# First batch of a packed attention and expert layer: the copy of T ahead of the gates' steps, row logits and guess one item back each

## The chip, the cores and the metric

One core of a Trainium2 chip runs the kernel. The metric is the device time of one execution in microseconds (us), lower is better. The engines are TensorE (PE, matmuls; PEld is its weight load), VectorE (DVE), ScalarE (ACT), GpSimd (POOL) and SyncE (SP, which issues most transfers). Each runs its instructions in the order in which the program gives them, and waits where an operand is not ready.

## The reference

Two attentions in a row, then a layer of experts. 32 packing queries `p` of each head attend to keys and values and give 32 packed rows; the queries `q` attend to these rows. The result (8 batches of 576 tokens, 512 wide) goes through a router that picks one of eight experts per token.

```python
p_packed = sm_attn(p, k, v)
out = sm_attn(q, p_packed, p_packed)
...
xn = x / (np.linalg.norm(x, axis=-1, keepdims=True) + 1e-06)
logits = xn @ en.T / tau
expert_idx = np.argmax(logits, axis=1)
gate_w = probs[np.arange(N), expert_idx]
h = np.maximum(x[mask] @ w1[e], 0.0)
out[mask] = gate_w[mask, None] * (h @ w2[e])
```

## The kernel before

The kernel works batch by batch (b = 0 to 7, 576 tokens each). For each batch it guesses one expert for all tokens, from the logits of the packed rows; it counts afterwards how many tokens chose another, and a loop at the end, which the drawn inputs do not enter, would handle those.

Attention of a batch: key scores, exponential, turning of the probabilities (`p1_turn`), packed rows (`pack_values`, L381), then two masked forms of these rows on DVE (`pair_rows`, `quad_rows`, L393). The pairs are turned on PE (`pair_turn`, L410) and **DVE copies them to T** (L474, in `att1`). T feeds three things on PE: the **row logits** (`row_logits`, L424), whose result DVE copies to m1 (L434), the **guess** (`guess`, L507: m1 with 1/tau), whose argmax DVE finds (L511 to L516) and which lets POOL issue the loads of the expert's weights (L730, L738), and the query scores (`query_scores`, L251). `att2` is the softmax on them: transposes (L547), largest (L552), shift (L558), exponential on ACT (L561), sum (L567), norm (L573), turning (L582), high and low half (L588 on ACT, L592 on DVE). After it DVE turns the next batch's keys (`keys`, L276 to L293). `route` (L644 on PE, L653 on DVE, L660 on ACT) gives the token's logits and the square of its norm, in five tiles that share two PSUM buffers `pt`; `counts` (L686, L691) counts the experts chosen.

`gates` turns a batch's norms and logits into a gate per token. It is a generator: four groups of three small DVE steps (the reciprocal square root, L89 to L108, then two closing steps, L703 and L704, in the fourth), then L706, L707, the exponential on ACT (L711), L714, L715, L717, L719. The gates are needed by the stores (`store_main`, L1139 on ACT, then the transfers of L1145).

`ffn` is the expert: first product (L840), rows of the last 64 tokens (L868), third product (L884: for each of four blocks of 128 tokens, eight steps f of three matmuls 128x512), each step followed by a `yield`. In the first batch a table of strings, `PLAN`, says what is put between these steps: item n+1 is run after yield n. In an item, a letter runs one step of a generator: `a` one step of the attention of batch 1, `g` one step of the gates of batch 0 (the first one starts them), `r` one of its route (nothing once that is over), `w` the split of a piece of the second weights. Items 28 to 35, which the change rewrites, stand around the first six steps f of the third product's first block: item 29 is run after f = 0, item 30 after f = 1, and so on. With items 30 and 31 the second masked rows of batch 1 are turned, T is copied, row logits and guess run and the query scores begin.

Batches 1 to 7 do not use the table; there a rule of steps per yield sets the order.

Of the kernel before, what the change touches and what calls it, by code (L numbers as in the profile page):

```python
# [23 lines left out]
def kernel(  # L24
# [1109 lines left out]
    def store_main(b):  # L1134
# [32 lines left out]
    PLAN = (  # L1167
        "qssq", "sssssssssq", "ssqsssG", "ss", "", "ss", "sa", "asss", "a", "Gsq",
        "ss", "", "a", "aswGG", "aa", "as", "w", "aw", "ag", "qaawas",
        "awa", "g", "", "", "arwrw", "", "ara", "arraar", "ararrrgw", "",  # L1170
        "gaa", "agaaaag", "", "ragraaararga", "a", "gar", "gr", "", "rggr", "r",
        "ra", "", "r", "gag", "gaga", "gagrar", "grara", "ag", "a", "grrgrar",
        "rrraggg", "", "g", "rr", "ggaaagr", "ra", "aaga", "g", "r", "rg",
        "arr",
# [75 lines left out]
    with tc.If(n_rest > 0):  # L1250
        with tc.For_i(0, B, 1) as b:
            nb = nc.values_load(rest_i[0:1, ds(b, 1)], min_val=0, max_val=S)
            with tc.If(nb > 0):
# [44 lines left out]
                for c in range(NC5):  # L1298
                    for hf in range(2):
                        a = acc[hf][:, c] if c < 4 else acc[0][64 * hf : 64 * hf + 64, 4]  # L1300
# [38 lines left out]
```

## Time and profile before

| | |
|---|---|
| median of 3 runs | 451.07 us (450.13 to 451.11) |
| the profiled execution | 450.72 us, of it span 449.0 us |
| PE busy | 433.0 us, 96% of the span, 3762 instructions |
| DVE busy | 307.9 us, 69%, 1020 instructions |
| ACT busy | 203.6 us, 45%, 477 instructions |
| POOL busy | 144.8 us, 32%, 184 instructions |
| granted clock of TensorE | 0.999 of full speed (2.4 GHz) on the mean |

The profile is one execution, with a start and a duration for each instruction, and for idle time what ended it. Starts are in us from the span's start. A timeline merges instructions of one kind that follow each other, so a row "x27" is 27 instructions. Successive instructions of an engine overlap a little in these records where they do not depend on each other. PE's matmuls are pipelined and their ends are modelled; the start of the next one tells more than the end of the last.

### The profile page before, as it was taken

How to read it: one execution, taken by the hardware profiler on the slowest of the kernel's cores; microseconds unless marked ns; L12 is line 12 of the kernel's file. 1: busy time of each engine (PE TensorE's matmuls, PEld its weight loads, DVE VectorE, ACT ScalarE, POOL GpSimd, SP SyncE). 2: the span in 40 equal slices, each digit the busy share in tenths (PEclk: the TensorE clock that was granted, in tenths of full speed). 3: DMA queues.
4: the chain of work that ended last, by engine and by line, in shares of the span. 5: the costliest groups of instructions: out<-in, count | busy, mean ns of one | idle time of the engine just before them, and what ended most of it. 6: DMA issues, size and time to landing. Idle time of an engine off the chain costs nothing.

```text
span 449.0 us, 10448 instructions
## 1 busy us (share of the span) xinstructions
PE 433.0 (96%) x3762; PEld 340.6 (76%) x3763; DVE 307.9 (69%) x1020; ACT 203.6 (45%) x477; POOL 144.8 (32%) x184
## 2 busy tenths in 40 slices
PE   8789989999999999999999999999999999999994
PEld 6527768788687878878687887879788796879784
DVE  4568879669874799459894699658894598545500
ACT  2456723575137622475226642377234751456111
POOL 2546723143404432143503423044411525035000
PEclk9999999999999999999999999999999999999999
DMA  7999979866993479933995289944898305600011
GB/s 207 283 262 296 232 208 324 260 157 183 307 333 107 129 212 368 269 104 109 294 361 166 77 215 317 295 124 112 237 391 224 97 1 187 247 26 23 15 47 53
DMA packets 40843, 88.22 MB, mean 196 GB/s; under 512 B 10376, under 2 KB 19912, under 8 KB 40784
## 3 DMA queue, kind: packets, MB, share of 16 engines
q1 hardware_dynamic: 32496, 57.96, 45.4%
q0 software_dynamic: 8000, 29.43, 17.9%
q8 instruction: 32, 0.52, 0.5%
q14 instruction: 27, 0.22, 0.2%
q10 hardware_dynamic: 288, 0.08, 0.1%
HBM read 78.00 MB, written 9.44 MB: 195 GB/s over the span
## 4 chain that ended last, share of the span: by engine, by line
PE 84%; DMA 5%; ACT 3%; DVE 3%; issue 2%; SPq 1%; ACTq 0%
PE pf L884 40%; PE pf L840 19%; PE pf L868 7%; PE pt L644 7%; PE pt L251 4%; PE pt L773 3%; PE pt L381 3%; DMA nat<-in_q 2%; ACT p L346 2%; DMA nat<-in_v 2%; DMA w1t<-in_moe_w 1%; PE pt L361 1%; DVE mx L341 1%; ACT w2s L748 1%; SPq L730 1%
## 5 line engine op out<-in xcount | busy, mean ns | idle before, releaser
L884 PE MATMUL pf<-w2s,hT 128*128 128x512 f32 (+1 forms) x792 | 188.3, 390 | 0.0
L884 PEld LDWEIGHTS pf<-w2s,hT 128*128 128x128 f32 x792 | 142.5, 188 | 37.7 <-issue 6.7
L749 POOL TENSOR_TENSOR w2s<-w2r,w2s 128x512 fp32r<-128x512 f32 x64 | 82.6, 1292 | 188.4 <-ACT w2s L748 187.6
L840 PE MATMUL pf<-AT,G 128*128 128x288 f32 x720 | 103.4, 298 | 0.0
L840 PEld LDWEIGHTS pf<-AT,G 128*128 128x128 f32 x720 | 97.4, 188 | 4.5 <-issue 3.3
L844 ACT ACTIVATE hT<-pf 128x224 fp32r<-128x224 f32 (+1 forms) x128 | 47.6, 385 | 48.4 <-PE pf L840 47.9
L845 DVE SCALAR_TENSOR_TENSOR hT<-pf,hT 128x224 fp32r<-128x224 f32 (+1 forms) x128 | 52.0, 410 | 18.7 <-ACT hT L844 18.2
L660 ACT ACTIVATE at<-pt 128x512 f32<-128x512 f32 (+1 forms) x40 | 23.9, 597 | 42.9 <-DVE lg L653 42.6
L748 ACT CAST w2s<-w2r 128x512 fp32r<-128x512 f32 x64 | 39.6, 620 | 1.2 <-issue 1.2
L1139 ACT ACTIVATE o<-pf,gate 128x512 f32<-128x512 f32 (+1 forms) x41 | 26.0, 634 | 30.9 <-PE pf L884 18.6
L644 PEld LDWEIGHTS pt<-ppx,AT 128*128 128x128 f32 (+1 forms) x240 | 33.0, 177 | 4.4 <-DVE p1T L375 0.4
L644 PE MATMUL pt<-ppx,AT 128*128 128x264 f32 (+1 forms) x240 | 35.4, 286 | 0.0
L868 PE MATMUL pf<-w2r,h 128*64 128x256 f32 x256 | 33.9, 390 | 0.0
L653 DVE TENSOR_REDUCE lg<-pt 128x8 f32<-128x16 f32 (+1 forms) x40 | 6.8, 171 | 38.2 <-PE pt L644 38.2
L281 DVE STREAM_TRANSPOSE kt<-nat 128x512 f32<-128x512 f32 x28 | 30.9, 1104 | 0.1
L787 DVE TENSOR_TENSOR G<-pt,G 128x512 fp32r<-128x512 f32 x28 | 18.8, 689 | 14.2 <-ACT G L786 14.2
L266 POOL TENSOR_TENSOR ppx<-pp,ppx 128x256 fp32r<-128x256 f32 x16 | 11.7, 754 | 40.4 <-ACT ppx L265 40.4
L561 ACT ACTIVATE st<-st 128x576 f32<-128x576 f32 (+1 forms) x17 | 11.2, 657 | 29.0 <-DVE st L558 28.3
L868 PEld LDWEIGHTS pf<-w2r,h 128*64 128x64 f32 x256 | 15.8, 136 | 9.9 <-issue 4.3
L738 POOL DMA_DIRECT2D w2r<-in_moe_w x28 | 19.7, 711 | 0.0
L588 ACT CAST AT<-at 128x576 fp32r<-128x576 f32 x16 | 10.7, 673 | 19.6 <-DVE at L582 19.6
L786 ACT CAST G<-pt 128x512 fp32r<-128x512 f32 x28 | 15.8, 588 | 7.1 <-DVE G L787 4.8
(172 smaller groups left out, 479.6 us busy)
## 6 DMA issues: line engine op xcount, KB each, us to landing
nat<-in_k SPq DMA_DIRECT2D x112, 140.0 KB, 3.4
nat<-in_q SPq DMA_DIRECT2D x112, 140.0 KB, 3.8
w1t<-in_moe_w POOLq DMA_DIRECT2D x14, 1024.0 KB, 7.6
w2r<-in_moe_w POOLq DMA_DIRECT2D x28, 512.0 KB, 10.4
out<-o SPq DMA_DIRECT2D x27, 256.0 KB, 2.7
nat<-in_v SPq DMA_DIRECT2D x32, 160.0 KB, 4.1
nat<-in_v SPq DMA_DIRECT2D x32, 128.0 KB, 4.0
w1t<-in_moe_w SPq DMA_DIRECT2D x8, 256.0 KB, 4.6
```

What stands on the lines that cost most here:

```text
L281: nc.vector.transpose(kt[:, :512].rearrange("p (c i a) -> p c a i", a=4, i=32), t[:, :16].rearrange("p (c a) d -> p c a d", a=4),)
L644: nc.tensor.matmul(pt[:r, 512 * g : 512 * g + XW], AT[:, a, g, c * P : c * P + r], x.ppx[:, m, g], start=(i == 0), stop=(i == 2),)
L660: nc.scalar.activation(scr[:r, :, : HB * D], ptv[:r, :, 0 : HB * D], AF.Square, accum_out=ss[:r, c : c + 1])
L738: queue.dma_start(t, w2e[:, 2 * i : 2 * i + 2, :])
L748: nc.scalar.copy(t[:, 0], raw)
L749: nc.gpsimd.tensor_tensor(out=t[:, 1], in0=raw, in1=t[:, 0].bitcast(F32), op=ALU.subtract)
L840: nc.tensor.matmul(pf[:, :HS], w, r, start=(n == 0), stop=(n == len(ops) - 1))
L844: nc.scalar.activation(hT[:, 0, f, cs], pf[:, :n], AF.Relu)
L845: nc.vector.scalar_tensor_tensor(out=hT[:, 1, f, cs], in0=pf[:, :n], scalar=0.0, in1=hT[:, 0, f, cs].bitcast(F32), op0=ALU.max, op1=ALU.su ...
L868: nc.tensor.matmul(pf[64 * hf : 64 * hf + 64, :256], h4[:, f], x.w2r[f // 2][:, f % 2, hf * 256 : hf * 256 + 256], start=(f == 0), stop=(f ...
L884: nc.tensor.matmul(pf[:, :w], hT[:, a, f, c * P : (c + 1) * P], x.w2s[f][:, m, at : at + w], start=(f == 0 and i == 0), stop=(f == NF - 1 ...
L1139: nc.scalar.activation(o[:, :w], pf[:, :w], AF.Copy, scale=x.gate[:, c : c + 1])
```

## The change

Items 28 to 35 of `PLAN` are rewritten. The number of `a` and `g` steps in the table stays the same, and no instruction is added or removed. The gates' first step moves from item 28 to item 32, the second from 30 to 33. The `a` steps that copy T stay in item 30; row logits move from item 31 to 32, guess and query scores from 31 to 33, and the softmax steps follow in 33 to 35.

```diff
-        "awa", "g", "", "", "arwrw", "", "ara", "arraar", "ararrrgw", "",
-        "gaa", "agaaaag", "", "ragraaararga", "a", "gar", "gr", "", "rggr", "r",
+        "awa", "g", "", "", "arwrw", "", "ara", "arraar", "ararrrw", "",
+        "aa", "", "ag", "aaag", "agaaaaga", "gaaa", "gr", "", "rggr", "r",
```

On PE, between the turning of the pairs (L410) and the rest of the third product's first block (L884), the order differs as follows (- before, + changed); `pu` holds the row logits and the guess, `pt` the query scores:

```order
-L884 MATMUL pf<-w2s,hT 128x512 x3
-L424 MATMUL pu<-enT,T 64x8 x4
-L507 MATMUL pu<-m_1015,itau 1x8 x2
-L251 MATMUL pt<-kt,T 32x288 x16
-L884 MATMUL pf<-w2s,hT 128x512 x69
+L884 MATMUL pf<-w2s,hT 128x512 x6
+L424 MATMUL pu<-enT,T 64x8 x4
+L884 MATMUL pf<-w2s,hT 128x512 x3
+L507 MATMUL pu<-m_1008,itau 1x8 x2
+L251 MATMUL pt<-kt,T 32x288 x16
+L884 MATMUL pf<-w2s,hT 128x512 x63
```

Six matmuls of the third product instead of three stand ahead of the row logits, three more between these and the guess, and six fewer behind the query scores.

On DVE, at the same place, from the counts of the first batch on, before (`rq_i`, `rq_h`, `rq_t` and `gy` are the gates' steps, `m_1015` is m1):

```order
L691 TENSOR_REDUCE cnt<-pu 1x8
L89 TENSOR_SCALAR rq_i<-ss 128x5
L93 TENSOR_SCALAR rq_i<-rq_i 128x5
L98 TENSOR_SCALAR rq_h<-ss 128x5
L103 TENSOR_TENSOR rq_t<-rq_h,rq_i 128x5
L105 TENSOR_TENSOR rq_t<-rq_t,rq_i 128x5
L108 SCALAR_TENSOR_TENSOR gy<-rq_t,rq_i 128x5
L474 COPY T<-pu 128x256
L434 COPY m_1015<-pu 128x16
L103 TENSOR_TENSOR rq_t<-rq_h,gy 128x5
L105 TENSOR_TENSOR rq_t<-rq_t,gy 128x5
L108 SCALAR_TENSOR_TENSOR gy<-rq_t,gy 128x5
```

And in the changed kernel, from the same counts to the argmax:

```order
L691 TENSOR_REDUCE cnt<-pu 1x8
L474 COPY T<-pu 128x256
L434 COPY m_1008<-pu 128x16
L89 TENSOR_SCALAR rq_i<-ss 128x5
L93 TENSOR_SCALAR rq_i<-rq_i 128x5
L98 TENSOR_SCALAR rq_h<-ss 128x5
L511 MAX m_1024<-pu 1x8
L512 MAX_INDEX idx<-m_1024,pu 1x8
L514 CAST gi<-idx 1x1
L516 TENSOR_SCALAR sel<-ecol,gi 1x8
L103 TENSOR_TENSOR rq_t<-rq_h,rq_i 128x5
L105 TENSOR_TENSOR rq_t<-rq_t,rq_i 128x5
```

The copies of T and m1 now stand directly behind the counts, ahead of all of the gates' steps; one group of three of those goes behind the score transposes.

On DVE, at the end of the gates, in the softmax of batch 1, before (`s_1099` and `mx_1094` are sums and largest values of the softmax):

```order
L706 RECIPROCAL gy<-gy 128x5
L707 TENSOR_TENSOR lg<-lg,gy 128x40
L567 TENSOR_REDUCE s_1099<-st 128x18
L568 TENSOR_SCALAR s_1099<-s_1099 128x18
L569 RECIPROCAL s_1099<-s_1099 128x18
L558 TENSOR_TENSOR st<-st,mx_1094 128x576
L714 TENSOR_REDUCE gate<-lg 128x5
L715 TENSOR_SCALAR gate<-gate 128x5
L573 TENSOR_TENSOR st<-st,s_1099 128x576
L717 RECIPROCAL gate<-gate 128x5
L719 COPY gate<-gate 64x1
```

And in the changed kernel (`s_1102` and `mx_1095` are the same two):

```order
L567 TENSOR_REDUCE s_1102<-st 128x18
L568 TENSOR_SCALAR s_1102<-s_1102 128x18
L569 RECIPROCAL s_1102<-s_1102 128x18
L558 TENSOR_TENSOR st<-st,mx_1095 128x576
L573 TENSOR_TENSOR st<-st,s_1102 128x576
L706 RECIPROCAL gy<-gy 128x5
L707 TENSOR_TENSOR lg<-lg,gy 128x40
L714 TENSOR_REDUCE gate<-lg 128x5
L715 TENSOR_SCALAR gate<-gate 128x5
L717 RECIPROCAL gate<-gate 128x5
L719 COPY gate<-gate 64x1
```

The reduction L714, which waits for ACT's exponential of `lg`, follows L707 directly, where four softmax steps stood between them; on ACT that exponential (L711) moves behind the second one of the softmax (L561). From the turning of the first half (L582) on, the order on DVE is the same in both, the keys of batch 2 ahead of the route reductions (L653) included; on SP nothing moves.

## Rows read from the trace of the kernel before

**Rows 1.** The waits of PE over the whole span: who waited for what, us in total, times, longest.

```profile
PE pu L424 <- DVE T L474: 1.1, 1, 1.1
PE pu L507 <- DVE m L434: 0.3, 1, 0.3
```

**Rows 2.** The timeline of PE from 61.75 to 66 us: start, us, engine, line, operation, tiles, count, and in brackets the idle time before it and what ended it.

```profile
61.75 0.38 PE L410 MATMUL pu<-ident,pp 128*128 128x128 f32 x2
61.89 0.95 PE L884 MATMUL pf<-w2s,hT 128*128 128x512 f32 x3
63.94 0.41 PE L424 MATMUL pu<-enT,T 128*64 128x8 f32 x8 [1.10 <-DVE T L474]
64.62 0.24 PE L507 MATMUL pu<-m,itau 128*1 128x8 f32 x4 [0.28 <-DVE m L434]
```

**Rows 3.** The timeline of DVE from 61.4 to 74 us, with the same columns.

```profile
61.44 0.18 DVE L691 TENSOR_REDUCE cnt<-pu 1x8 f32<-1x40 f32 x1
61.54 0.15 DVE L89 TENSOR_SCALAR rq_i<-ss 128x5 int32<-128x5 int32 x1
61.73 0.74 DVE L93 TENSOR_SCALAR rq_i<-rq_i 128x5 int32<-128x5 int32 x1
...
62.58 0.58 DVE L103 TENSOR_TENSOR rq_t<-rq_h,rq_i 128x5 f32<-128x5 f32 x1
...
63.47 0.42 DVE L474 COPY T<-pu 128x256 f32<-128x256 f32 x1
64.39 0.17 DVE L434 COPY m<-pu 128x16 f32<-128x16 f32 x1 [0.51 <-PE pu L424]
...
66.19 0.84 DVE L547 STREAM_TRANSPOSE st<-pt 128x288 f32<-128x288 f32 x2
...
67.11 0.17 DVE L704 TENSOR_SCALAR gy<-gy 128x5 f32<-128x5 f32 x1
...
73.94 0.76 DVE L582 STREAM_TRANSPOSE at<-st 128x576 f32<-128x576 f32 x1
```

**Rows 4.** Two lines of the gates on DVE over the whole span, from the view of one source line: count, then shortest, median and longest duration in ns.

```profile
L93 DVE TENSOR_SCALAR rq_i<-rq_i x9: 99/172/745, 9.7 to 417.8; 128x5 int32<-128x5 int32 x8, 8x1 int32<-8x1 int32 x1
...
L103 DVE TENSOR_TENSOR rq_t<-rq_h,rq_i x8: 165/166/578, 62.6 to 418.0; 128x5 f32<-128x5 f32 x8
```

**Rows 5.** The timeline of POOL in the first batch's stretch, and its weight issues in the next batch (last row).

```profile
61.70 1.43 POOL L266 TENSOR_TENSOR ppx<-pp,ppx 128x256 fp32r<-128x256 f32 x2 [1.03 <-ACT ppx L265]
...
67.08 1.58 POOL L730 DMA_DIRECT2D w1t<-in_moe_w  x2 [1.96 <-DVE gy L703]
68.65 2.83 POOL L738 DMA_DIRECT2D w2r<-in_moe_w  x4
...
114.86 1.51 POOL L730 DMA_DIRECT2D w1t<-in_moe_w  x2 [2.20 <-DVE rq_t L105]
```

**Rows 6.** The timeline of DVE from 78 to 84 us: the low half of the second part of the softmax, and the first route reduction behind the keys.

```profile
78.67 0.76 DVE L592 TENSOR_TENSOR AT<-at,AT 128x576 fp32r<-128x576 f32 x1 [0.74 <-ACT AT L588]
...
83.01 0.17 DVE L653 TENSOR_REDUCE lg<-pt 128x8 f32<-128x16 f32 x1
```

**Rows 7.** The timeline of ACT: the gates' exponential, the first route tile's square with the reading of its sum, and the reading of the fourth one's.

```profile
70.70 0.24 ACT L711 ACTIVATE lg<-lg 128x40 f32<-128x40 f32 x1 [1.25 <-DVE lg L707]
...
83.77 0.19 ACT L660 ACTIVATION_READ_ACCUMULATOR at<-pt 128x1 f32 x1
...
87.36 0.19 ACT L660 ACTIVATION_READ_ACCUMULATOR at<-pt 128x1 f32 x1
```

**Rows 8.** The timeline of PE from 75.8 to 90 us: the third product's end, the route tiles (L644) and the first product's rows of the next batch (L773).

```profile
75.80 6.44 PE L884 MATMUL pf<-w2s,hT 128*128 128x512 f32 x27
82.08 1.63 PE L644 MATMUL pt<-ppx,AT 128*128 128x264 f32 x12
...
84.24 0.90 PE L644 MATMUL pt<-ppx,AT 128*128 128x264 f32 x6
...
87.61 1.95 PE L773 MATMUL pt<-w1t,T 64*32 64x512 f32 x32 [0.33 <-ACT at L660]
```

**Rows 9.** The timeline of DVE in the second batch, from 113 to 117 us: the guess's MAX, gate steps, and the gate reduction.

```profile
113.10 0.15 DVE L511 MAX8 m<-pu 1x8 f32<-1x8 f32 x1
...
113.87 0.15 DVE L103 TENSOR_TENSOR rq_t<-rq_h,gy 128x5 f32<-128x5 f32 x1
...
114.45 0.17 DVE L103 TENSOR_TENSOR rq_t<-rq_h,gy 128x5 f32<-128x5 f32 x1
...
114.85 0.17 DVE L108 SCALAR_TENSOR_TENSOR gy<-rq_t,gy 128x5 f32<-128x5 f32 x1
...
115.25 0.35 DVE L704 TENSOR_SCALAR gy<-gy 128x5 f32<-128x5 f32 x1
...
116.42 0.20 DVE L714 TENSOR_REDUCE gate<-lg 128x5 f32<-128x40 f32 x1 [0.36 <-ACT lg L711]
```

**Rows 10.** The waits of PE from 84 us to the end of the span, all that this view shows, in the form of rows 1.

```profile
PE pt L361 <- ACT p L346: 2.1, 6, 0.4
PE pt L773 <- ACT at L660: 0.3, 1, 0.3
```

**Rows 11.** The longest standstill of PE on a weight transfer, in the timeline, and the stretch of 26 to 28 us in the table of stretches (stretch, its length, then busy us and instructions of PE, PEld, DVE, ACT and POOL, granted clock, share of the transfer engines, GB/s).

```profile
28.27 1.05 PE L808 MATMUL pf<-w1t,tw 64*32 64x512 f32 x4 [1.29 <-DMA w1t<-in_moe_w]
...
26.00:28.00 2.00, 0.98 (x6) 0.07 (x4) 1.97 (x4) 1.61 (x4) 0.94 (x2) 1.00 1.00 340
```

## Prediction

> **What bounds the kernel now.** I read the waits of TensorE (PE) first, then the chain and timelines of the stretch that the change touches. PE is busy 96% of the span, so time comes out of its waits or nowhere. Two of these lie together in the first batch: 1.1 us in which the row logits wait for the copy of T, and 0.3 us in which the guess waits for the copy of m1 [rows 1]. The timeline shows the place: between the turning of the pairs and the query scores PE does three matmuls, then stands still [rows 2]. VectorE (DVE) was the late one: after the counts it ran six gate steps before the copy of T, which began at 63.47 [rows 3], although the turned pairs were there at 61.75 + 0.38 = 62.13 [rows 2]. Two of the six were slow, 0.74 and 0.58 us [rows 3], against medians of 0.17 over the run [rows 4]; GpSimd (POOL) was running its own split from 61.70 to 63.13 [rows 5].
>
> The second thing to see is twenty microseconds on. From the query scores DVE runs softmax, gates and the turning of the next batch's keys almost without a pause, and only then, at 83.01, the reduction of the first route tile [rows 6]. ScalarE (ACT) squares that tile up to 83.77 + 0.19 = 83.96 [rows 7], and the third route tile on PE, which takes over its buffer, starts at 84.24 [rows 8]. In the kernel before, PE comes there 0.28 us after the buffer is free. DVE is thus nearly the bound of this stretch, though PE looks full.
>
> **What PE gains.** No instruction is added or taken away; PE's row logits go behind two more steps of the third product, the guess behind one more. At the rate of 27 matmuls from 75.80 to 82.08 [rows 8], 0.233 us each, six take 1.40 us from 61.89: the row logits start at 63.29, after T is there (62.13 + 0.04 + 0.42 = 62.59). The handover of 0.04 is that from the row logits' end to the copy of m1, 64.35 to 64.39 [rows 2, 3]. Both waits of PE go: 1.10 + 0.28 = 1.38 us. PE therefore reaches the first route tiles at about 80.7 instead of 82.08.
>
> **What DVE pays.** The same instructions run, but with other idle time. T starts at 62.17 (idle 0.55, from the counts' end at 61.62). The copy of m1 needs the row logits: 63.29 + 0.41 + 0.04 = 63.74, so DVE stands idle from 62.59 to there, 1.15 us, with the gates queued behind it. The first gate group then runs in the clear of POOL and is some 0.57 us shorter; the second sheds 0.41 as well [rows 3, 4]. The guess ends at 63.29 + 0.41 + 3 x 0.233 + 0.24 = 64.64 if nothing overlaps; I take 64.6 for the MAX behind it. From MAX to the transposes of the scores stand the same instructions, in the same order, as from MAX to the last step of the second batch: 113.10 to 114.85, plus the 0.08 after which a next, independent instruction starts, as from 61.44 + 0.18 to 61.54 [rows 3, 9]. That is 1.83 us, and the transposes start at 66.43, not 66.19: 0.24 late, although PE had the scores ready.
>
> From the transposes to the turning of the first half took 66.19 to 73.94, 7.75 us [rows 3]. Into this stretch come: one group of three gate steps, 113.87 to 114.45 or 0.58 [rows 9]; the wait of the gate reduction for ACT's exponential, 0.36 in the second batch [rows 9], where the kernel before had other DVE work between them (the exponential at 70.70, [rows 7]); and 0.18 because the addition of L704 now falls among POOL's weight issues. In the first batch it ran before them in 0.17, in the second among them in 0.35 [rows 3, 5, 9]. Sum 1.12. POOL's issues start at 67.08 and last until 71.48 [rows 5]; L704 would come at about 70.9, so I count this in full. The turning is late by 0.24 + 1.12 = 1.36 us.
>
> **What is late next.** From there to the first route reduction the order is the same, and every step hangs on the one before (the low half of the second product waits for ACT too, 0.74, and shifts with it [rows 6]). So the reduction comes at 83.01 + 1.36, ACT is done at 85.32, and the third route tile starts 0.06 later (as L773, which began at 87.61 behind ACT's 87.55 [rows 7, 8]), at 85.38 instead of 84.24. PE's 1.38 us are a longer wait in front of this tile: it would be there at about 82.9 and stands for some 2.5 us. The end of the program moves by 85.38 - 84.24 = **+1.14 us**, since all behind it (third product, L773, the second batch) hangs on PE or on the same ACT and DVE chain, and from 84 us to the end PE waits only for ACT, not for a transfer that would come at its own time and take the shift up [rows 10]. The first store waits for the gates and starts later by as much; SyncE is not full between the first and the second store, and the second follows ACT's work anyway. POOL gets the guess about 0.3 us sooner and issues the weights sooner, which nobody waits for; I cost both at nothing.
>
> Against the profiled execution: 450.72 + 1.14 = 451.9 us; that execution lies 0.35 below the median of 451.07, so 452.2 us, 0.25% slower.
>
> **Bounds of the unknown pieces.** MAX could start at 64.2 if PE overlaps more (-0.4); the three steps may hide in the transposes (-0.12); L704 may run clear (-0.18); the wait for the exponential may be up to 0.2 longer, and three pairs that used to have other work between them may cost 0.1 each. The lateness of DVE is then 0.66 to 1.86, that of PE 0.4 to 1.6 us: 451.5 to 452.7. The runs shown differ by up to 0.98, of which I add about a half below and a quarter above.
>
> **What a rule would make of L704.** The row shows 0.35 against 0.17. The Trainium skill, SBUF — State Buffer, section "Who interferes with whom", says that a VectorE operation in a two-port mode and a GpSimd operation shut each other out for a whole instruction. By that rule the price could be the rest of a weight issue and not 0.18, and the sum would go up to that of the first rival below. The case's rows bear out the exclusion (0.74 and 0.58 under POOL's split), but in the one row that has L704 among weight issues only 0.18 was lost.
>
> **The rivals.** *Slower beyond what can be measured* (other side of the bound): L704 waits out a whole weight issue, 2.83 / 4 = 0.71 us [rows 5], in place of 0.18, with all of softmax queued behind it on DVE. DVE is then 1.89 late, PE 1.67: 452.7 us. It decides when DVE is over 1.6 late. For it: the two slow steps of [rows 3]; against: the 0.35 of [rows 9].
>
> *Almost no change*: DVE is late by 0.7 or less, since work overlaps that I laid end to end; PE's gain turns into a wait and the end moves by at most 0.5: 451.3 us. For it: every term is small, and some may hide.
>
> *The gain is kept*: if route tiles didn't wait for DVE, 1.38 us would remain: 449.7 us. The wait of 84.24 would have to vanish, and the 0.28 us of slack says that DVE must not get later at all. The order of keys before route reduction is unchanged, which speaks against it.
>
> *The clock falls*: PE would stand for 2.5 us in front of the third route tile. In this trace it stood 1.29 us before 28.27 with a granted clock of 1.00 (2.4 GHz) in that stretch [rows 11], and no longer standstill is shown once it runs. If the clock fell to 1.2 GHz, matmuls that take 0.233 us would take 0.466, and some 2 us of work would cost 2 more: 454.2 us. The Trainium skill, TensorE: Matmul & The Clock Gate, section "What's actually happening", says that an idle array drops to half rate; the row of 1.29 us shows no drop, and a standstill of 2.5 us is shown by no run yet.
>
> **How the numbers follow.** A measurement of this kernel tells about 0.3%, 1.35 us, from no change. Forecast (+0.5 to +1.35): 0.51. L704 or the like, beyond +1.35: 0.27. Almost no change: 0.15. Gain kept: 0.04. Clock: 0.03. Hence faster 0.04, same 0.51 + 0.15 = 0.66, slower 0.27 + 0.03 = 0.30. The range of 451.0 to 453.0 holds the forecast, nearly all of the third case and most of the first rival, and leaves out the rest.
>
> **What the profile after would show.** PE: the waits at L424 and L507 gone, the route tiles reached near 80.7, then a wait of 2 to 2.5 us for ACT's square in front of the third. DVE: T at 62.2, m1 at 63.7 after about 1.1 us idle, no slow step in the gates' first two groups, transposes at 66.4, the turning at 75.3, the first route reduction at 84.4. If the reduction came at 83.0 or sooner, the account of DVE would be wrong; if PE did not wait at the third tile, the bound would be.

## The result, and the profile after

| | before | changed | ratio (95% interval) |
|---|---|---|---|
| first measurement, median | 450.86 us (7 runs) | 453.0 us (7 runs) | 1.0053 (1.0028 to 1.0078) |
| second measurement (e0) | 451.36 us (35 runs) | 453.31 us (12 runs) | 1.0047 (1.0021 to 1.0072) |
| third measurement (e8) | 451.38 us (35 runs) | 452.78 us (12 runs) | 1.0037 (1.0009 to 1.0064) |
| profiled execution, span | 449.0 us | 451.4 us | |

The changed kernel is slower, by about twice what was forecast (450.86 x 0.0053 = 2.4 us against 1.14). The measured 453.0 lies 0.8 us above the forecast time of 452.2, at the upper end of its range, and the forecast that no change could be told was wrong: no interval contains 1. The mechanism that it named is in the trace, line by line, and a second one, to which it had given a chance of 0.03, is there in some profiles.

In the profile after, PE had waited less for the first weights (0.8 us in all instead of 1.9, at L808): its counts are reduced at 60.71 instead of 61.44, so 0.73 is to be added to its starts before they are set beside those of [rows 2] to [rows 8]. The timeline of PE, in the form of [rows 2] and [rows 8]:

```profile
61.03 0.38 PE L410 MATMUL pu<-ident,pp 128*128 128x128 f32 x2
61.16 1.64 PE L884 MATMUL pf<-w2s,hT 128*128 128x512 f32 x6
62.73 0.41 PE L424 MATMUL pu<-enT,T 128*64 128x8 f32 x8
63.07 0.96 PE L884 MATMUL pf<-w2s,hT 128*128 128x512 f32 x3
63.96 0.24 PE L507 MATMUL pu<-m,itau 128*1 128x8 f32 x4
...
80.01 1.63 PE L644 MATMUL pt<-ppx,AT 128*128 128x264 f32 x12
81.48 0.87 PE L884 MATMUL pf<-w2s,hT 128*128 128x512 f32 x3
84.88 1.33 PE L644 MATMUL pt<-ppx,AT 128*128 128x264 f32 x6 [2.53 <-ACT at L660]
86.00 1.48 PE L884 MATMUL pf<-w2s,hT 128*128 128x512 f32 x3
...
89.85 1.95 PE L773 MATMUL pt<-w1t,T 64*32 64x512 f32 x32 [0.29 <-ACT at L660]
```

Both waits of [rows 1] are gone: no bracket stands at L424 and L507. PE reaches the route tiles at 80.01 + 0.73 = 80.74, 1.34 us sooner. Then it stands 2.53 us in front of the third one, which starts at 84.88 + 0.73 = 85.61 instead of 84.24. The timeline of ACT shows why: the square of the first tile waits for DVE's reduction of it, and PE starts 0.06 us after the reading of its sum (84.63 + 0.19 = 84.82).

```profile
84.14 0.60 ACT L660 ACTIVATE at<-pt 128x512 f32<-128x512 f32 x1 [3.95 <-DVE lg L653]
84.63 0.19 ACT L660 ACTIVATION_READ_ACCUMULATOR at<-pt 128x1 f32 x1
```

The timeline of DVE, in the form of [rows 3] and [rows 6]:

```profile
60.71 0.18 DVE L691 TENSOR_REDUCE cnt<-pu 1x8 f32<-1x40 f32 x1
61.44 0.42 DVE L474 COPY T<-pu 128x256 f32<-128x256 f32 x1 [0.56 <-PE pu L410]
63.19 0.17 DVE L434 COPY m<-pu 128x16 f32<-128x16 f32 x1 [1.32 <-PE pu L424]
...
63.48 0.17 DVE L93 TENSOR_SCALAR rq_i<-rq_i 128x5 int32<-128x5 int32 x1
...
64.24 0.16 DVE L511 MAX8 m<-pu 1x8 f32<-1x8 f32 x1 [0.52 <-PE pu L507]
...
66.08 0.84 DVE L547 STREAM_TRANSPOSE st<-pt 128x288 f32<-128x288 f32 x2
...
70.48 0.29 DVE L704 TENSOR_SCALAR gy<-gy 128x5 f32<-128x5 f32 x1
...
73.79 0.20 DVE L714 TENSOR_REDUCE gate<-lg 128x5 f32<-128x40 f32 x1 [0.36 <-ACT lg L711]
...
74.90 0.76 DVE L582 STREAM_TRANSPOSE at<-st 128x576 f32<-128x576 f32 x1
...
83.91 0.21 DVE L653 TENSOR_REDUCE lg<-pt 128x8 f32<-128x16 f32 x2
```

T, m1 and MAX each stand behind an idle time now (0.56, 1.32, 0.52), where the kernel before had gate steps and 0.51 of idle time. The slow L93 of 0.74 takes 0.17. From the counts to the first route reduction DVE needs 83.91 - 60.71 = 23.20 us instead of 83.01 - 61.44 = 21.57: **1.63 us more**. The waits of PE from 60 us to the end, in the form of [rows 10]:

```profile
PE pt L644 <- ACT at L660: 2.5, 1, 2.5
PE pt L361 <- ACT p L346: 2.2, 6, 0.4
PE pt L773 <- ACT at L660: 0.3, 1, 0.3
```

One new line has come, and it is larger than the two that went. The table of stretches around it, in the form of [rows 11] (the third number from the right is the granted clock):

```profile
82.00:84.00 2.00, 0.35 (x2) 0.00 (x0) 2.00 (x10) 0.00 (x0) 0.00 (x0) 1.00 0.68 192
84.00:86.00 2.00, 1.12 (x6) 1.12 (x7) 0.12 (x2) 1.86 (x6) 0.53 (x1) 0.83 0.91 267
86.00:88.00 2.00, 2.00 (x8) 1.71 (x8) 0.17 (x1) 1.19 (x3) 0.75 (x1) 0.50 0.99 271
88.00:90.00 2.00, 1.71 (x18) 1.45 (x25) 0.47 (x3) 0.83 (x3) 0.00 (x0) 0.81 0.98 247
```

PE did almost nothing from 82 to 84 (0.35 us), and after that the granted clock fell from 1.00 to 0.50 of full speed, the lower of its two levels (1.2 GHz). The three matmuls from 86.00 took 1.48 us instead of the 0.87 of those from 81.48.

**A length that holds still.** Times of whole executions scatter by up to 6 us (449.07 to 455.06 for the kernel before). Much of that lies ahead of the change: in the profiles the first counts come between 58.41 and 62.31, PE has waited up to 3.4 us for weights at L808 until then, and in 7 of the 14 profiles the granted clock has fallen at least once in the first 32 us. So the clock alone, which the expectation of e11 names, does not explain them: e8, without one, reaches the counts at 61.35, the changed kernel, with one, at 59.26. Beside the measured time I read from each profile one stretch: from the start of the counts' matmuls in the first batch (L686) to that in the second. Behind it all kernels take 355.7 to 356.3 us to the end of the span.

| kernel | first counts | second counts | stretch | clock in it |
|---|---|---|---|---|
| before | 59.99 | 93.26 | 33.27 | 1.00 |
| before again (e11) | 58.41 | 91.70 | 33.29 | 1.00 |
| changed | 59.26 | 95.51 | 36.25 | falls near 85 |
| changed again (e0) | 59.31 | 95.45 | 36.14 | falls near 86 |
| changed, third (e8) | 61.35 | 96.08 | 34.73 | 1.00 |
| spare matmuls (e1, e9) | 62.31, 61.63 | 97.06, 96.37 | 34.75, 34.74 | 1.00 |
| keys between (e2) | 59.33 | 91.36 | 32.03 | 1.00 |
| gates in the waits (e3) | 61.13 | 94.35 | 33.22 | 1.00 |
| T first alone (e4) | 60.52 | 93.91 | 33.39 | 1.00 |
| late logits alone (e5) | 60.56 | 94.29 | 33.73 | 1.00 |
| before, keys between (e6) | 59.97 | 94.90 | 34.93 | falls near 66 |
| both (e7) | 59.33 | 91.37 | 32.04 | 1.00 |
| before, spare matmuls (e10) | 60.20 | 93.47 | 33.27 | 1.00 |

### The profile page after: what moved, and what is told of

The parts are those of the page before. It is cut to its first block, busy times and chain, and to the rows that moved or that the text cites. A ratio compares the mean times of both kernels' runs of the same rounds, so it can differ in the third digit from the quotient of the medians.

```text
span 451.4 us, 10448 instructions
## 1 busy us (share of the span) xinstructions
PE 435.6 (97%) x3762; PEld 342.6 (76%) x3763; DVE 307.5 (68%) x1020; ACT 203.6 (45%) x477; POOL 145.3 (32%) x184
## 4 chain that ended last, share of the span: by engine, by line
PE 81%; DMA 7%; DVE 5%; ACT 4%; issue 2%; SPq 1%; DVEq 0%; ACTq 0%
PE pf L884 37%; PE pf L840 18%; PE pf L868 7%; PE pt L644 6%; PE pt L251 3%; PE pt L773 3%; PE pt L381 3%; ACT p L346 2%; DMA w1t<-in_moe_w 2%; DMA nat<-in_k 2%; DMA nat<-in_v 2%; DMA nat<-in_q 1%; PE pt L361 1%; DVE mx L341 1%; ACT w2s L748 1%
## 5 line engine op out<-in xcount | busy, mean ns | idle before, releaser
L884 PE MATMUL pf<-w2s,hT 128*128 128x512 f32 (+1 forms) x792 | 189.3, 391 | 0.0
L884 PEld LDWEIGHTS pf<-w2s,hT 128*128 128x128 f32 x792 | 142.7, 189 | 37.9 <-issue 6.7
L644 PEld LDWEIGHTS pt<-ppx,AT 128*128 128x128 f32 (+1 forms) x240 | 33.9, 183 | 7.3 <-ACT at L660 3.0
L644 PE MATMUL pt<-ppx,AT 128*128 128x264 f32 (+1 forms) x240 | 36.5, 292 | 2.5 <-ACT at L660 2.5
L653 DVE TENSOR_REDUCE lg<-pt 128x8 f32<-128x16 f32 (+1 forms) x40 | 6.7, 169 | 39.7 <-PE pt L644 39.7
L561 ACT ACTIVATE st<-st 128x576 f32<-128x576 f32 (+1 forms) x17 | 11.2, 658 | 32.7 <-DVE st L558 32.0
```

The lines of the kernel that those rows point to most:

```text
L644: nc.tensor.matmul(pt[:r, 512 * g : 512 * g + XW], AT[:, a, g, c * P : c * P + r], x.ppx[:, m, g], start=(i == 0), stop=(i == 2),)
L884: nc.tensor.matmul(pf[:, :w], hT[:, a, f, c * P : (c + 1) * P], x.w2s[f][:, m, at : at + w], start=(f == 0 and i == 0), stop=(f == NF - 1 ...
```

## The experiments

The theory after the result: DVE's lateness reaches PE through the third route tile and costs about 1.4 us; the fallen clock costs 1.5 more. Rival A: only the clock costs. Rival B: late gates make the stores late, and these cost. For the later runs, theory C says that the clock falls behind PE's standstill in every execution, theory D that it falls in some. The edits show of `PLAN` only the items around the change. Each kernel was measured in 12 executions beside 35 of the kernel before.

**e0, the changed kernel again.** No edit.

> The changed kernel once more, so that the next three have it on the same chip. My theory now: VectorE comes 1.6 to 1.7 us later to the first route reduction, PE stands 2.5 us in front of the third route tile, and after that standstill the granted clock falls to half for some 3.4 us of work, which costs 1.6 us more. Expected: 452.5 to 454, with a stretch at a granted clock of 0.5 near 85 to 88 us. Rival A (the whole loss is the clock, the late VectorE alone would cost nothing) and rival B (the loss comes from stores and transfers that start later behind the late gates) give the same time here.

Measured: 453.31 us; its profile stands 2.53 us before the third tile, and the clock falls there too.

**e1 and e9, work in the standstill.** Spare matmuls in front of the third route tile (their result is not read):

```diff
-"ggaaagr", "ra", "aaga"
+"ggaaagr", "dra", "aaga"
...
+                if c == "d":
+                    pf = ps.tile([P, 512], F32, name="pd", tag="pf")
+                    t = bat[0].w2s[0][:, 0]
+                    for _ in range(9):
+                        nc.tensor.matmul(pf, t[:, :P], t, start=True, stop=True)
...
```

> The changed kernel with nine spare matmuls 128x512 (their result is not read) on PE directly ahead of the third route tile, where PE stands for 2.5 us; they take about 2.1 us and end before the wait does. My theory: the wait still ends when ScalarE frees the buffer, at the same time, but the clock stays at 1.00, and 1.4 to 1.6 us of the loss are gone: 451.2 to 451.8, still 0.3 to 1.0 above the kernel before. Rival A: the kernel gets as fast as the kernel before or faster by PE's 1.4 us: 449.5 to 450.8. Rival B: no change, 453.

> The changed kernel with the nine spare matmuls again. In its first profile the stretch from counts to counts took 34.75 us with the clock at 1.00, but the median was 453.28, no lower than that of the changed kernel, with a granted clock that had fallen twice in the first 32 us. Expected of the stretch: 34.7 to 34.8. Theory C expects the median 1.4 us below that of the changed kernel (451.6 to 452.0), theory D 0.5 to 1.0 below. Equal medians over both calls would say that the clock behind the standstill costs nothing in the timed executions.

The timeline of PE in e1:

```profile
85.22 2.24 PE L1210 MATMUL pd<-w2s 128*128 128x512 f32 x9
87.92 1.00 PE L644 MATMUL pt<-ppx,AT 128*128 128x264 f32 x6 [0.46 <-ACT at L660]
...
91.40 1.95 PE L773 MATMUL pt<-w1t,T 64*32 64x512 f32 x32 [0.29 <-ACT at L660]
```

and the stretch behind the third tile's start:

```profile
88.00:90.00 2.00, 2.00 (x14) 1.86 (x15) 0.17 (x1) 2.00 (x6) 1.29 (x1) 1.00 0.99 278
```

The wait shrinks to 0.46, the tile starts as late as ever, and the clock stays at 1.00. The stretch is 34.75 and 34.74 us: the late VectorE costs 1.47 us against 33.28 with the clock up. That refutes rival A in the profile. The times did not follow: 453.28 us (1.0031, 1.0012 to 1.0051) and 453.25 (1.0032, 1.0005 to 1.0059), not the 451.2 to 451.8 expected of e1, nor the 0.5 us or more below the changed kernel that theories C and D both had for e9. Over all executions the changed kernel has a median of 453.23 (31), that with spare matmuls 453.25 (24); the means, 453.21 and 453.09, are 0.13 us apart, with a 95% interval of about -0.5 to +0.8 us from the scatter of both. So a fall in every execution, at 1.5 us each, does not fit the times, if the spare matmuls keep the clock up in the timed executions as they do in both profiles; a fall in some of them does, and so does none at all.

**e8, the changed kernel a third time.**

> The changed kernel a third time, with more executions, beside the next one on the same chip. From the counts of the first batch to those of the second the two profiles so far took 36.25 and 36.14 us, the kernel before 33.27: 1.5 of the 2.9 us more lie in the stretch at half clock behind the standstill of 2.53 us. If the clock falls there in every execution (theory C): 36.1 to 36.3 again, and a median of 453.0 to 453.5. If it falls in some executions only (theory D), this profile may show 34.7.

Measured: 452.78 us. PE in its profile:

```profile
86.96 1.00 PE L644 MATMUL pt<-ppx,AT 128*128 128x264 f32 x6 [2.52 <-ACT at L660]
...
90.43 1.95 PE L773 MATMUL pt<-w1t,T 64*32 64x512 f32 x32 [0.28 <-ACT at L660]
```

and the stretch behind the same standstill, with the clock in the third number from the right:

```profile
86.00:88.00 2.00, 1.04 (x7) 1.03 (x8) 0.21 (x3) 1.78 (x6) 0.45 (x1) 1.00 0.97 262
88.00:90.00 2.00, 2.00 (x15) 1.72 (x13) 0.35 (x2) 1.47 (x5) 0.84 (x1) 1.00 0.96 264
```

The same wait, 2.52 us, and no fall. So theory C falls, and in the profiles theory D holds: the clock falls in some executions and not in others. Without it the stretch is 34.73 us, 1.46 more than the 33.27 of the kernel before.

**e2, keys between the route reductions.** In the second batch `keys` and `route` run step by step beside each other; PLAN is that of the change:

```diff
-        second = att2(x, keys_main(b + 1) if b else None, b == 0, b < 1)
+        split = b == 1
+        second = att2(x, keys_main(b + 1) if b and not split else None, b == 0, b < 1)
...
-        if b:
+        if split:
+            yield from idle(5)
+            live = [route(x), keys_main(b + 1)]
+            while live:
+                live = [g for g in live if next(g, True) is None]
+                if live:
+                    yield
+        elif b:
             yield from route(x)
```

The five idle steps stand where the five steps of `keys` stood, so that PE's order stays that of the change.

> The changed kernel, but in the second batch the turning of the next keys on VectorE stands between the route reductions instead of ahead of all of them; PE's order and the gates' order are as in the change. My theory: the first route reduction no longer waits for 3.5 us of key transposes, no standstill of PE over 0.5 us remains in front of the route tiles, the clock stays up, and PE keeps its 1.4 us: 449.2 to 449.8, faster than the kernel before. Rival A: the same, or less by the clock's share alone (451.4). Rival B: the gates and the stores are as late as in the change, so 452.5 to 453.

The timeline of DVE:

```profile
80.37 0.22 DVE L292 TENSOR_SCALAR pbd<-pn 128x128 f32<-128x128 f32 x1
...
81.01 0.17 DVE L653 TENSOR_REDUCE lg<-pt 128x8 f32<-128x16 f32 x1
81.19 0.45 DVE L276 STREAM_TRANSPOSE kt<-nat 128x256 f32<-128x256 f32 x1
...
82.01 0.13 DVE L653 TENSOR_REDUCE lg<-pt 128x8 f32<-128x16 f32 x1
```

and of PE:

```profile
80.08 1.63 PE L644 MATMUL pt<-ppx,AT 128*128 128x264 f32 x12
...
82.25 0.90 PE L644 MATMUL pt<-ppx,AT 128*128 128x264 f32 x6
...
85.61 2.04 PE L773 MATMUL pt<-w1t,T 64*32 64x512 f32 x32 [0.32 <-ACT at L660]
```

DVE is as late as in the change (80.37 against 80.30 at L292), but the first reduction follows 0.64 us behind that instead of 3.61 (83.91 - 80.30), and the third tile has no wait. Measured: 449.90 us, just above the expected range, ratio 0.9969 (0.9945 to 0.9992), **faster than the kernel before**; stretch 32.03, 1.24 us shorter. The gates are as late as in the change, so rival B falls. Nor does the changed kernel lose noticeably behind the stretch, where late stores would show: 355.9 to 356.3 us there in its three profiles, 355.7 and 355.9 in those of the kernel before.

**e3, gates in DVE's waits.** The edit is against the change; row logits and guess stay as there:

```diff
-"aa", "", "ag", "aaag", "agaaaaga", "gaaa",
+"aa", "gg", "ag", "aaag", "agaaaaga", "gaaa",
```

> The changed kernel with the copy of T still first, but two groups of the gates' steps in the wait of VectorE between T and m1, and one between m1 and the argmax; row logits, guess and PE's order are as in the change. My theory: VectorE's transposes of the scores start 0.5 us earlier than in the change and the group behind the second ones is gone, so the first route reduction is 0 to 0.5 us later than in the kernel before instead of 1.6; PE waits 0.8 to 1.5 us for the third route tile, too short for the clock to fall: 450.6 to 451.4, the time of the kernel before. Rival A: faster than the kernel before by up to 1.4 us. Rival B: gates are nearly as early as before, so about the time of the kernel before as well.

Measured: 451.16 us, ratio 0.9989 (0.9964 to 1.0014). The wait in front of the third tile is 0.99 us, the stretch 33.22: with DVE nearly on time again (23.11 us from the first counts on PE to the first reduction, 23.02 before) PE's gain is given back to the last tenth, and no loss comes on top. The section on the change says that the number of `g` steps in the table stays the same. That is not so: items 28 to 35 have seven before and five in the changed kernel, and the later items are unchanged. The same gate instructions run, but later items run them, and this is why a group and the closing steps fall so late into the softmax. e3 puts the two back, and L714 comes 10.68 us behind the first counts on PE (71.81 - 61.13) instead of 14.53 (73.79 - 59.26).

**e4, T first alone.** Row logits and guess unmoved, five `g` as in the change (the edit is shown against the kernel before):

```diff
-"ararrrgw", "", "gaa", "agaaaag", "", "ragraaararga", "a", "gar",
+"ararrrw", "", "aa", "agaaaag", "", "ragraaararga", "a", "gar",
```

> The first half of the change alone: the copy of T ahead of the gates' steps, row logits and guess where they stood before. My theory: PE's 1.1 us in front of the row logits go, the 0.3 us in front of the guess stay. VectorE starts the score transposes some 1.3 us earlier but has two gate groups and the wait for the exponential in the softmax, so the first route reduction comes at about its old time, and PE waits there 1 to 1.4 us instead: 450.5 to 451.3, no change. If PE's waits alone counted: 449.7.

PE in its profile:

```profile
63.30 0.41 PE L424 MATMUL pu<-enT,T 128*64 128x8 f32 x8
63.98 0.25 PE L507 MATMUL pu<-m,itau 128*1 128x8 f32 x4 [0.28 <-DVE m L434]
...
84.77 1.00 PE L644 MATMUL pt<-ppx,AT 128*128 128x264 f32 x6 [1.01 <-ACT at L660]
```

Measured: 450.90 us, ratio 0.9990 (0.9967 to 1.0014). The 1.10 us have moved from L424 to the third route tile, almost one for one.

**e5, late row logits and guess alone.** Seven `g`, the first two ahead of T (against the kernel before):

```diff
-"gaa", "agaaaag", "", "ragraaararga", "a", "gar",
+"gaa", "", "ag", "aaag", "agaaaaga", "gaaa",
```

> The second half alone: gates' first two groups ahead of T as before, row logits and guess one item back as in the change. My theory: T is there at its old time, PE does three more matmuls meanwhile and waits some 0.5 us instead of 1.1; nothing waits for the guess. The first route reduction is 0.3 us late, PE's lead of about 1 us is lost there: 450.8 to 451.5. If PE's waits alone counted: 450.0.

Measured: 451.84 us, above the 450.8 to 451.5 expected, ratio 1.0006 (0.9984 to 1.0027); the wait for T is 0.43, that before the third tile 1.00, the stretch 33.73, 0.46 longer. The first reduction was 0.60 us late (84.18 - 60.56 against 83.01 - 59.99) where 0.3 had been expected: MAX stood idle for 0.42 behind the guess, a wait that I had not counted in full.

**e6 and e7, keys between in the kernel before, and with e3.** The edit of e2 on the kernel before, and on e3.

> The kernel before, with the turning of the next keys between the route reductions. My theory: PE had 0.28 us to spare there and one wait of 0.33 us behind it, so at most that wait goes: 450.4 to 450.9. A gain of over 1 us here would say that the key transposes bound the kernel before as well, and that my reading of the slack is wrong.

> Gates' groups in the waits and keys between the route reductions together, with PE's order of the change. My theory: no wait is left in the stretch but the start-up of the route tiles; PE keeps its 1.4 us and the wait of 0.33 us: 449.0 to 449.6, about as the run with the keys moved alone.

e6: 452.08 us, above the 450.4 to 450.9 expected, ratio 1.0011 (0.9985 to 1.0037): no gain, so the keys did not bound the kernel before. The profile says the same without the scatter: from the first route tile to the second counts it takes 94.90 - 83.62 = 11.28 us, the kernel before 93.26 - 82.08 = 11.18. Its wait of 0.33 at L773 did not go either (0.32), though I had expected that it would. Its profile shows the clock falling behind the kernel before's own wait for T:

```profile
64.00:66.00 2.00, 1.72 (x44) 0.97 (x44) 1.42 (x11) 0.20 (x1) 0.24 (x1) 0.79 0.90 240
66.00:68.00 2.00, 2.00 (x19) 1.16 (x4) 1.48 (x7) 0.00 (x0) 0.94 (x2) 0.50 0.11 35
```

e7: 449.84 us, above the 449.0 to 449.6 expected, ratio 0.9967 (0.9939 to 0.9994), stretch 32.04: the same as e2. With the reduction freed of the keys, it makes no difference here where the gates stand.

**e10 and e11, the kernel before with spare matmuls in its wait for T, and again.** The edit of e1 with five matmuls and `"dagaaaag"` in place of `"agaaaag"`.

> The kernel before with five spare matmuls 128x512 (1.2 us, result not read) in PE's wait for T. One profile with the kernel before's order at this place showed the clock at half from about 65 to 69 us, behind PE's waits of 1.10 and 0.28 us, and a stretch from counts to counts of 34.93 us; the profile of the kernel before itself showed neither (33.27). Expected: clock at 1.00 there, stretch of 33.2 to 33.4. If the kernel before loses clock at its own wait in a third of the executions, the median falls by about 0.5: 450.5 to 451.0 against the 451.3 of the kernel before; if it never does: equal.

> The kernel before once more, for a second profile of it and its scatter. Expected: ratio 1.000 within its interval; stretch from counts to counts 33.3 if the clock stays up behind the wait for T, 34.9 if it falls. Its median of 451.3 and lowest and highest of 449.1 and 455.1 in earlier runs come from the first 60 us, where the clock falls in some executions before the change begins.

e10: 450.89 us, 0.9994 (0.9972 to 1.0017); e11: 450.84, 0.9998 (0.9975 to 1.0021). Both have the clock at 1.00 at this place and 33.27 and 33.29 us. Whether the kernel before loses clock there often can't be told from this: half a microsecond is within the interval.

## Why the prediction was wrong

**What held.** PE's gain: 1.38 forecast, 1.34 found at the first route tiles (six matmuls ahead of the row logits are two steps of the third product, one more than before, not two more; the sum had them right). DVE's bill in kind: idle time in front of T (0.55 forecast, 0.56), the clear run of L93, the wait for the exponential (0.36, 0.36), L704 slowed (0.18, and 0.29 - 0.17 = 0.12). From MAX to the turning of the first half I had 75.30 - 64.6 = 10.70; the trace has 74.90 - 64.24 = 10.66. And the place where it is paid: the wait of 2 to 2.5 us in front of the third tile came as 2.53. That this tile hangs on DVE is shown by e2, where it lost its wait as soon as DVE's reduction came earlier, and by five profiles of four kernels in which the reduction and the tile both moved: 83.91 and 84.88 (changed), 83.95 and 84.92 (e0), 84.24 and 85.21 (e3), 83.81 and 84.77 (e4), 84.18 and 85.16 (e5): 0.96 to 0.98 apart each time.

The Trainium skill, SBUF — State Buffer, section "Who interferes with whom", has a VectorE operation in a two-port mode and a GpSimd operation shut each other out for a whole instruction; L93 fell from 0.74 to 0.17 when it left POOL's split, which agrees, though no run shows the mode that it ran in. L704 among the weight issues lost 0.12, not a whole issue of 0.71, so the first rival's price did not come. Its condition did, by another way: DVE was over 1.6 us late (1.69). The weight issues, which the prediction had 0.3 us sooner, began at 66.37 + 0.73 = 67.10 against 67.08, which cost nothing.

**The first step that failed** is a term of DVE's bill: "I take 64.6 for the MAX behind it". From L410 to the row logits PE took 62.73 - 61.03 = 1.70 us, where I had 1.54 by the steady rate of 0.233; from there to the guess 1.23, where I had 1.11; and MAX began 0.28 after the guess, where 64.6 had left 0.20. DVE's idle time in front of m1 was 1.32 instead of 1.15 for the same reason. MAX stood at 64.24 + 0.73 = 64.97, 0.37 late, and all of softmax behind it. DVE was 1.69 late at the turning instead of 1.36, PE 1.37 instead of 1.14 at the third tile and 1.46 at the second counts (e8). The rate of a long row of equal matmuls did not hold for six of them between turnings and row logits; what slowed them no run shows. The bounds of the prediction let MAX come earlier only (64.2), not later. Its 0.08 between the last gate step and the transposes was right (66.00 to 66.08), although the row that it names has 0.10 (61.44 to 61.54).

**The second** is the chance of 0.03 for the falling clock. Its reason, a standstill of 1.29 us with no fall, told nothing about 2.5 us. The stretch that it shows also ends at 28.00, before the standstill does at 28.27; the one behind it has the clock up too:

```profile
28.00:30.00 2.00, 1.54 (x8) 0.31 (x8) 1.53 (x5) 1.07 (x2) 1.58 (x2) 1.00 1.04 256
```

Two of three profiles of the changed kernel show the fall, worth 36.2 - 34.73 = 1.5 us there, less than the 2 us for which the prediction had no row; the third does not. The Trainium skill, TensorE: Matmul & The Clock Gate, section "What's actually happening", speaks of an idle array that drops to half rate; the trace agrees, though three equal standstills gave two falls.

**The sum.** 1.46 us is 0.32% of 451 us, just beyond the 0.3% that I had set as the bound for slower, and it lies in all three intervals. The medians point to 1.4 to 2.1 us. Whether the part above 1.46 is clock, lost in some executions, or scatter isn't settled: the spare matmuls, which kept the clock up in both profiles, did not lower the median. No run tells whether they shift the fall elsewhere.

## What to carry to other kernels

A wait that is removed from the busiest engine is worth only what the next engine has to spare: here VectorE had 0.28 us of slack twenty microseconds on, and whatever came above that turned into a wait there. Moving work behind a copy so that the copy runs first leaves idle time in front of each later step that hangs on the copy's users; put independent work into exactly these waits (e3), or take the work off the path that the next bound lies on (e2, which made the same change a gain of 0.3%). Where whole executions scatter, a stretch between two landmarks of the trace tells tenths of a microsecond that medians of twelve do not.

## What the runs showed of the hardware that was not expected

The granted clock fell to half behind a standstill of 2.53 us in two profiles and did not behind 2.52 us in a third; behind waits of 1.10 and 0.28 us with 0.4 us of work between, it fell in one profile (e6) and not in two others (the kernel before, e11), nor in e10, where the first of the waits was filled. In every profile with single waits of 0.99 to 1.01 us before the third tile (e3, e4, e5) it stayed at 1.00. A fall cost 1.4 to 1.7 us each time (36.14 and 36.25 against 34.73; 34.93 against 33.27).
